# Twelve units: the products of P with the values, and the 64-row products of their items, in quarters of the array

## The chip, the cores and the metric

The kernel runs on one core of a Trainium2 chip. The time is device microseconds (us) of one execution. A profile is one such execution taken by the hardware profiler; it lists every instruction with start and duration, and its span runs from the first to the last of them.

## The reference

An mLSTM cell is followed by a feed-forward layer. The cell has 4 batch rows, 8 heads, 768 tokens and 40 features a head. For each token, with a running maximum m of the gates,

```
m_new  = max(f + m, i);  fs = exp(f + m - m_new);  is = exp(i - m_new)
C      = fs * C + is * v k^T        (40 x 40 a head)
nvec   = fs * nvec + is * k
y      = sigmoid(o) * (C q) / max(|nvec . q|, 1)
```

The outputs of all heads, 320 features a token, make x with 3072 rows. Then h = x @ w_in (320 x 2048), g = h - tanh(h), out = g @ w_out (2048 x 320), all in float32.

## The kernel before, in words

**Units.** The recurrence is cut into chunks of 128 tokens. A unit is one chunk of one batch row; there are 24. Within a unit the cell becomes matmuls: scores `ps` = k q (by head, masked to the causal half and kept as P in SBUF, 128 key tokens by 128 query tokens), P times the scaled values `vs` (whose 41st column is the scaled ones of the normaliser), plus the old state times q. A product of keys and values, `pc`, updates the state for the same batch row's next chunk.

**Items.** The feed-forward runs in items: a group of two units (256 tokens) with one or two pairs p of 128-wide blocks of the 2048 hidden features. `up` (L1015) makes h of an item: w_in's 320 rows are cut in 128, 128 and 64, so each of the two blocks of a pair gets two full products of 128 rows (`full`) and one of 64 rows. The 64-row ones (`rest`) of the two blocks lie in the upper and the lower half of the array's rows and run at the same time. `shrink_steps` (L1036) evaluates g from the PSUM banks ph0 and ph1 by ScalarE (`z`, `q`) and VectorE (`gt`); `sums_of_g` (L888) makes four sums `s1` to `s4` of quarters of g on VectorE, so that `down_seven` (L903) does the second product with seven instead of eight block products, in the banks `pS`. The second product of an item is done while the next item is under way (`LAG` = 1).

**Two schedules.** Units 0 to 11 and the items of the first four groups are ordered by a planner (`Plan`, L157) with a cost for each step. From the item `START` = 17 on, a plain loop (L1497) writes out each item: the full products of `up`, then its 64-row products and, in every other item, the scores of the next unit (L1506), then the second product of the item before. Steps of other engines are put between by a counted clock (`Clock.later`, L141), and each engine runs its instructions in exactly this order.

**Units 12 to 23.** They run in the loop, one in two items. In the item after its scores, a unit gets `block_turned` (L764) between the 64-row products and the second product. It computes the cell's output turned round (features on partitions, tokens along the row) in two banks `turned[0]`, `turned[1]` (`pT` in the profile), one for each half of the heads. Its three parts on TensorE:

- eight products of the old state with q: 40 rows, 64 columns, one in each quarter of the array at a time (L772 to L777);
- eight products of the values with P: 128 rows, 64 columns, so two at a time, in the two column halves (L778 to L784);
- eight products for `pc`, 128 rows and 64 columns too, unless the chunk is the last of its batch row (L785 to L792). Units 20 to 23 have none.

At 1.2 us of the counted clock after that, `turn_back` (L801) transposes both banks in blocks of 32 x 32 on VectorE into `zt`, and SyncE's queue sends them through DRAM (`h_rows`) and reads them back as tokens by features (`z_in`). `gate_turned` (L819) divides and gates in the next unit's slot, and `turn_by_store` (L735) takes the result through DRAM to `xT`. `keep_halves` (L794) updates the state.

**What sets the order on TensorE.** All its instructions are chained in program order (`T.keep`, L120), so a product that waits holds up all that follow. A float32 matmul of the program shows as two MATMUL and two LDWEIGHTS records. The helper lines L106, L129 and L133 record all instructions, so the profile is read by tiles: `ph_up` (item's first product), `pT` (turned output), `pc`, `pS` (second product), `s` and `gt` as above.

Of the kernel before, what the change touches and what calls it, by code (L numbers as in the profile page):

```python
# [49 lines left out]
FP = mybir.dt.float32  # L50
# [5 lines left out]
OP = mybir.AluOpType  # L56
# [4 lines left out]
L = 128  # L61
# [18 lines left out]
def kernel(  # L80
# [33 lines left out]
    V, A, SP, G = Pinned(nc.vector), Pinned(nc.scalar), Pinned(nc.sync), Pinned(nc.gpsimd)  # L114
# [155 lines left out]
    D1 = D + 1  # L270
# [6 lines left out]
    NK = 2  # L277
    HALF = 64
# [6 lines left out]
    HH = H // 2  # L285
# [11 lines left out]
    NX = FIRST + 2  # L297
# [4 lines left out]
    att = ctx.enter_context(tc.tile_pool(name="att", bufs=2))  # L302
# [4 lines left out]
    ps_a = ctx.enter_context(tc.tile_pool(name="ps_a", bufs=1, space=PSUM))  # L307
# [4 lines left out]
    def small(shape, name):  # L312
        banks.append(banks.pop(0))
        return ps_b.tile(shape, FP, name=name, tag=banks[-1])
# [5 lines left out]
    w_in = const.tile([128, NP, WP], FP, name="w_in")  # L320
# [3 lines left out]
    xT = [const.tile([128, NK + 1, TG], FP, name=f"xT{i}") for i in range(NX)]  # L324
# [256 lines left out]
    un = {}  # L581
# [72 lines left out]
    def halves(*parts):  # L654

        for first in (0, 1):
            for steps in parts:
                for step in steps[first]:
                    step()
# [72 lines left out]
    BLOCK = 32  # L732
# [31 lines left out]
    def block_turned(n):  # L764

        t = un[n]
        G.memset(t["wide"][:, H * D1:], 0.0)
        t["turned"] = [ps_a.tile([128, 2, L], FP, name="pT", tag=f"a{i}") for i in range(2)]  # L770
        old = state[t["b"]][(t["c"] + 1) % 2].rearrange("p h d -> p (h d)")
        for g in range(2):  # L772
            for c in range(2):
                for i in range(2):
                    rows, j = slice(i * HALF, i * HALF + D), 2 * g + c
                    T.matmul(t["turned"][i][c * HALF:(c + 1) * HALF, g, :], old[rows, j * D1:j * D1 + HALF], t["qz"][rows, j, :],
                             start=(g == 0), stop=False, skip_group_check=True)  # L777
        for i in range(2):  # L778
            for g in range(2):
                for c in range(2):  # L780
                    j = 2 * g + c
                    at = (i * HH + j) * D1
                    T.matmul(t["turned"][i][c * HALF:(c + 1) * HALF, g, :], t["wide"][:, at:at + HALF], t["P"][:, i, j, :],
                             start=False, stop=True, skip_group_check=True)  # L784
        if n + B < NU:  # L785
            t["pc"] = small([128, HH, D1], "pc")
            k_flat = t["k"].rearrange("p h d -> p (h d)")
            for j in range(HH):
                for i in range(2):
                    h = i * HH + j  # L790
                    T.matmul(t["pc"][i * HALF:(i + 1) * HALF, j, :], k_flat[:, h * D:h * D + HALF], t["vs"][:, h, :],
                             start=True, stop=True, skip_group_check=True)  # L792
# [8 lines left out]
    def turn_back(n):  # L801


        t = un[n]
        zt = att.tile([128, HH * L // BLOCK, BLOCK], FP, name="zt", tag="P", bufs=4)
        flat = zt.rearrange("p b i -> p (b i)")
        for i in range(2):
            V.transpose(flat[:, i * 2 * L:(i + 1) * 2 * L], t["turned"][i].rearrange("p g t -> p (g t)"))
        rows = dram.tile([2, 2, HH, L, BLOCK], FP, name="h_rows", tag=f"h_rows{n % 4}")
        for a in range(128 // BLOCK):  # L810
            half, low = divmod(a, 2)
            SP.dma_start(out=rows[low, half].rearrange("g (b k) i -> k (g b) i", k=BLOCK), in_=zt[a * BLOCK:(a + 1) * BLOCK])
        t["z"] = att.tile([L, 2, H, BLOCK], FP, name="z_in", tag="P", bufs=4)
        for i in range(4):
            part = slice(i * BLOCK, (i + 1) * BLOCK)
            SP.dma_start(out=t["z"][part].rearrange("t a h i -> t (a h) i"),
                         in_=rows.rearrange("a c g t i -> t (a c g) i")[part])
# [55 lines left out]
    def in_seven(g, p):  # L873

        return g >= FIRST or p >= SPLIT
# [136 lines left out]
        r0 = row_of(n)  # L1012
        Clock.later("sent", wait, lambda: A.dma_start(out=out[r0:r0 + L, :], in_=ob))

    def up(some, shrink):  # L1015

        n = len(some)
        ph = [ps_h.tile([128, 2, TG], FP, name="ph_up", tag=f"ph{i}") for i in range(2)]

        def product(i, x, j):  # L1020
            g, p = some[x]
            f = 2 * p + i
            at = ((0, 2, 1), (0, 1, 2))[i][j]
            if j < NK:
                col = (i, 3 - i)[j]
                lhs, rhs = w_in[:, p, col * 128:(col + 1) * 128], xT[g % NX][:, at, :]
            else:
                rows = slice(i * HALF, (i + 1) * HALF)
                lhs, rhs = w_in[rows, p, 2 * NK * 128:], xT[g % NX][rows, at, :]
            T.matmul(ph[i][:, x, :], lhs, rhs, start=(x == 0 and j == 0), stop=(j == NK), skip_group_check=True)  # L1030

        full = [(0.43, lambda i=i, x=x, j=j: product(i, x, j)) for i in range(2) for x in range(n) for j in range(NK)]
        rest = [lambda i=i, x=x: product(i, x, NK) for x in range(n) for i in range(2)]
        return full, (rest, [lambda: shrink(some, ph)])

    def shrink_steps(x, some, ph):  # L1036
# [45 lines left out]
    def shrink(x):  # L1082
        def steps(some, ph):
            n = len(some)
            square, again, cube, product = shrink_steps(x, some, ph)
            for step in (square, again):
                for i in range(2):
                    step(i)
            for i in range(2):
                Clock.later(some, 0.9 + 0.35 * n * i, lambda i=i: cube(i))  # L1090
                Clock.later(some, 1.0 + 0.75 * n + 0.35 * n * i, lambda i=i: product(i))
            if x == len(items) - 1:
                Clock.later("count", 1.0 + 0.36 * n, over_bound)
            if in_seven(*some[0]):
                Clock.later(some, 1.01 + 1.1 * n, lambda: sums_of_g(some))

        return steps
# [56 lines left out]
    while sum(map(len, items)) < len(pairs):  # L1154
        x = sum(map(len, items))
# [64 lines left out]
    of_tokens, of_states, exponentials, rows = {}, {}, [], []  # L1220
# [131 lines left out]
    for p in range(SPLIT, NP):  # L1352
        steps = []
        op = None
        for i in range(2):
            op = plan.add("V", 0.65, lambda p=p, i=i, steps=steps: [steps.extend([] if i else sums_of_weights(p)), *[step() for _, step in steps[2 * i:2 * i + 2]]],
                          [op] if op else [converted[p, 1], *([made[p - 1]] if p % 2 else [converted[n, k] for n in range(1, NP) for k in range(2)])], -7.7512 + -3.8283 * p)
        made[p] = op

    def plan_item(x):  # L1360
# [6 lines left out]
        def begin_item():  # L1367
            busy.append(x)
            got.extend(up(some, lambda some, ph: got.append(shrink_steps(x, some, ph))))
# [109 lines left out]
    def spread_over(steps, x0, x1):  # L1479

        for i, (cost, step) in enumerate(steps):
            at = x0 + i * (x1 - x0) / len(steps)
            work[int(at)].append((at, cost, step))
# [13 lines left out]
    for x in range(START, len(items) + LAG):  # L1497
        dense, new, scored = [], [], news
        for slot, x0, x1 in begins[x]:
            spread_over(cell_slot(*slot), x0, x1)  # L1500
            if slot[0] is not None:
                new.append(slot[0])
        if x < len(items):
            some = tuple(run[:2] for run in items[x])
            dense, rest = up(some, shrink(x))
            dense.append((0.6 + 0.9 * len(new[:1]), lambda: halves(rest, *(scores(n) for n in new[:1]))))  # L1506
            for n in scored:
                dense.append((1.9, lambda n=n: [block_turned(n), Clock.later("turned", 1.2, lambda: [turn_back(n), n + B < NU and keep_halves(n)])]))
        dense += [(0.9, lambda n=n: halves(scores(n))) for n in new[1 if x < len(items) else 0:]]
        some = tuple(run[:2] for run in items[x - LAG])  # L1510
        if in_seven(*some[0]):
            dense += down_seven(some)
        else:
            for i, run in enumerate(items[x - LAG]):
                dense += down(i, some, *run)
        if x == len(items):
            dense.insert(4, (0.0, count))
            dense.insert(13, (0.0, load_count))
        news = new
        merge(dense, [(at - x, cost, step) for at, cost, step in sorted(work[x], key=lambda w: w[0])])  # L1520
# [87 lines left out]
    lead, root, _, rest = POLY  # L1608
# [17 lines left out]
    with tc.If(loaded[0] > 0):  # L1626
# [17 lines left out]
        for g in range(NG):  # L1644
# [19 lines left out]
            for p0 in range(0, NP, 2):  # L1664
# [5 lines left out]
                for p in (p0, p0 + 1):  # L1670
                    for i in range(2):
                        for tt in range(GT):
                            T.matmul(ob[tt], gts[i][:, p - p0, tt * L:(tt + 1) * L], w_out[:, 2 * p + i, :],
                                     start=(p == 0 and i == 0), stop=(p == NP - 1 and i == 1))
# [45 lines left out]
```

## Time and profile before

| what | value |
|---|---|
| median of 3 runs | 521.77 us (521.42 to 532.6) |
| the profiled execution's own time | 523.67 us |
| its span, first to last instruction | 522.0 us |
| TensorE busy (PE) | 512.8 us, 98% |
| VectorE busy (DVE) | 368.4 us, 71% |
| ScalarE busy (ACT) | 200.6 us, 38% |
| granted TensorE clock, mean | 0.995 |

In the profile, PE is TensorE's matmuls and PEld its weight loads. A line of a timeline gives the start, the length, the engine, and how many records of one kind follow each other; "128*64 128x128" is 128 rows and 64 columns of weights and a moving operand of 128 partitions by 128. A busy TensorE is not one at its peak: what counts is the distance between the starts of successive matmuls, since they are pipelined.

### The profile page before, as it was taken

Reading aid. Unit: us, or ns where it says so; the run is one execution under the profiler, and the core shown is the slowest. Engines: PE = TensorE matmul, PEld = TensorE weight load, DVE = VectorE, ACT = ScalarE, POOL = GpSimd, SP = SyncE. Lnnn points to the kernel's source line nnn. Section 1 sums busy time; section 2 is a strip of 40 time slices with the busy share of each in tenths; the row PEclk is TensorE's granted clock in tenths of the full one; section 3 lists DMA queues with packets and bytes.
Section 4 is the critical chain, followed back from the end, with each engine's and each line's share of the span. In section 5 each row is a group of like instructions: output and inputs, shape, how many; then the busy total and the mean of one; then the engine's idle time right before and its main releaser. Section 6 shows DMA issues by size and latency. Waiting matters only on the chain.

```text
span 522.0 us, 9917 instructions
## 1 busy us (share of the span) xinstructions
PE 512.8 (98%) x3705; PEld 442.4 (85%) x3705; DVE 368.4 (71%) x828; ACT 200.6 (38%) x511; POOL 38.3 (7%) x75
## 2 busy tenths in 40 slices
PE   9999999999999999999999999999999999999995
PEld 5778888887898888898898898898888888898984
DVE  5899979998855657786767667668658658663734
ACT  4465697676434242231321331232232232232321
POOL 5423224120000000000000000000000000000000
PEclk9899999999999999999999999999999999999999
DMA  7987646431003000042533533534433432310001
GB/s 228 285 245 227 180 141 193 131 111 33 3 3 91 6 27 26 4 108 50 133 64 89 147 67 85 129 69 87 107 77 85 107 79 36 80 31 1 26 1 31
DMA packets 100383, 47.29 MB, mean 91 GB/s; under 512 B 75048, under 2 KB 94056, under 8 KB 100328
## 3 DMA queue, kind: packets, MB, share of 16 engines
q1 hardware_dynamic: 94096, 31.84, 25.3%
q0 software_dynamic: 3040, 10.82, 6.6%
q10 hardware_dynamic: 3192, 3.93, 2.2%
q8 instruction: 31, 0.51, 0.4%
q14 instruction: 24, 0.20, 0.1%
HBM read 36.91 MB, written 9.44 MB: 89 GB/s over the span
## 4 chain that ended last, share of the span: by engine, by line
PE 94%; DMA 3%; ACT 1%; POOL 1%; DVE 0%; issue 0%; SPq 0%; DVEq 0%
PE ph_up L129 42%; PE pS L129 31%; PE po L129 7%; PE ph L129 4%; PE pT L129 4%; PE ps L129 4%; PE pc L129 2%; DMA w<-in_moe_w_in 2%; PE px L133 1%; DMA w_out<-in_i_gate 0%; POOL w L106 0%; ACT vs L106 0%; PE awake L129 0%; ACT L106 0%; DVE w_in L106 0%
## 5 line engine op out<-in xcount | busy, mean ns | idle before, releaser
L129 PE MATMUL ph_up<-xT,w_in 128*128 128x256 f32 (+1 forms) x1152 | 228.9, 388 | 0.0
L129 PEld LDWEIGHTS ph_up<-xT,w_in 128*128 128x128 f32 (+1 forms) x1152 | 176.2, 189 | 35.5 <-issue 15.3
L106 ACT ACTIVATE z<-ph_up 128x512 f32<-128x512 f32 (+1 forms) x98 | 56.8, 583 | 254.2 <-issue 123.7
L106 DVE SCALAR_TENSOR_TENSOR gt<-ph_up,z 128x512 f32<-128x512 f32 (+1 forms) x98 | 63.5, 675 | 68.0 <-ACT z L106 67.6
L129 PE MATMUL pS<-wT,s 128*128 128x160 f32 x480 | 72.0, 299 | 0.0
L129 PEld LDWEIGHTS pS<-wT,s 128*128 128x128 f32 x480 | 67.4, 190 | 0.0
L106 ACT ACTIVATE q<-z,tiny 128x512 f32<-128x512 f32 (+1 forms) x98 | 66.3, 711 | 1.0
L106 DVE SCALAR_TENSOR_TENSOR gt<-q,gt 128x512 f32<-128x512 f32 (+1 forms) x98 | 63.2, 676 | 0.0
L106 DVE TENSOR_TENSOR P<-ps,upto 128x512 f32<-128x512 f32 x36 | 23.3, 686 | 52.9 <-PE ps L129 52.8
L129 PE MATMUL pS<-w_out,gt 128*128 128x160 f32 x320 | 54.3, 312 | 0.0
L129 PEld LDWEIGHTS pS<-w_out,gt 128*128 128x128 f32 x320 | 44.6, 189 | 7.5 <-issue 3.6
L129 PE MATMUL po<-w_out,gt 128*128 128x320 f32 x128 | 38.2, 441 | 0.0
L129 PEld LDWEIGHTS po<-w_out,gt 128*128 128x128 f32 x128 | 23.1, 190 | 8.5 <-issue 0.3
L106 DVE TENSOR_TENSOR s<-gt 128x256 f32<-128x256 f32 x80 | 30.2, 418 | 0.0
L129 PE MATMUL pS<-w_out,s 128*128 128x160 f32 x160 | 28.3, 299 | 0.0
L129 PE MATMUL pS<-wT,gt 128*128 128x160 f32 x160 | 28.3, 299 | 0.0
L129 PEld LDWEIGHTS ps<-qz,kz 40*128 40x128 f32 x384 | 25.7, 190 | 2.1 <-issue 0.7
L129 PE MATMUL ps<-qz,kz 40*128 40x128 f32 x384 | 26.5, 276 | 0.0
L129 PEld LDWEIGHTS ph<-vs,P 128*128 128x128 f32 x192 | 23.9, 192 | 1.6 <-POOL P L106 1.2
L129 PE MATMUL ph<-vs,P 128*128 128x41 f32 x192 | 24.4, 273 | 0.7 <-POOL P L106 0.7
L129 PEld LDWEIGHTS pS<-w_out,s 128*128 128x128 f32 x160 | 23.9, 190 | 0.0
L129 PEld LDWEIGHTS pS<-wT,gt 128*128 128x128 f32 x160 | 23.9, 190 | 0.0
(105 smaller groups left out, 475.6 us busy)
## 6 DMA issues: line engine op xcount, KB each, us to landing
w<-in_moe_w_out POOLq DMA_DIRECT2D x8, 640.0 KB, 6.2
w<-in_moe_w_in POOLq DMA_DIRECT2D x16, 256.0 KB, 4.7
kz<-in_kT SPq DMA_DIRECT2D x48, 80.0 KB
o<-in_o_gate SPq DMA_DIRECT2D x24, 160.0 KB
k<-in_k SPq DMA_DIRECT2D x20, 180.0 KB
qz<-in_qT SPq DMA_DIRECT2D x44, 80.0 KB
v<-in_v SPq DMA_DIRECT2D x22, 160.0 KB
out<-ob ACTq DMA_DIRECT2D x11, 320.0 KB
```

The source lines that it names most:

```text
L106: i = method(*args, **kwargs)
L129: return cls.keep(nc.tensor.matmul(*args, **kwargs))
L133: return cls.keep(nc.tensor.transpose(*args, **kwargs))
```

## The change

It touches four places, for units 12 to 23 and their items alone.

- `block_turned`: the products of the values with P are cut along the key tokens in two halves of 64 rows, sixteen instead of eight, each in a quarter of the array. The bank now goes by the token half r, so each of the two banks has four blocks (head half i and g) instead of two, and the state's products go where they were by partition, at block `i * 2 + g`. The sum over the token halves is no longer made in PSUM.
- `update_halves`: the part of `block_turned` that makes `pc`, as a function of its own; nothing else changes in it.
- `turn_back`: ScalarE copies bank 1 (128x512) to SBUF, VectorE adds bank 0 to it, and one transpose of 128x512 takes the place of two of 128x256. The new buffer `both` holds `zt` and the sum; it is as large as the other tiles of its tag `P`.
- `up`: a new argument `quarters`. In the items where a unit has its `block_turned` (`scored` not empty), each 64-row product of 64x128 is made as two of 64x64, one for each column half.

```diff
+        t["turned"] = [ps_a.tile([128, 2 * 2, L], FP, name="pT", tag=f"a{i}") for i in range(2)]
         for g in range(2):
             for c in range(2):
                 for i in range(2):
                     rows, j = slice(i * HALF, i * HALF + D), 2 * g + c
-                    T.matmul(t["turned"][i][c * HALF:(c + 1) * HALF, g, :], old[rows, j * D1:j * D1 + HALF], t["qz"][rows, j, :],
+                    T.matmul(t["turned"][i][c * HALF:(c + 1) * HALF, i * 2 + g, :], old[rows, j * D1:j * D1 + HALF], t["qz"][rows, j, :],
                              start=(g == 0), stop=False, skip_group_check=True)
         for i in range(2):
             for g in range(2):
                 for c in range(2):
-                    j = 2 * g + c
-                    at = (i * HH + j) * D1
-                    T.matmul(t["turned"][i][c * HALF:(c + 1) * HALF, g, :], t["wide"][:, at:at + HALF], t["P"][:, i, j, :],
-                             start=False, stop=True, skip_group_check=True)
+                    for r in range(2):
+                        rows, j = slice(r * HALF, (r + 1) * HALF), 2 * g + c
+                        at = (i * HH + j) * D1
+                        T.matmul(t["turned"][r][c * HALF:(c + 1) * HALF, i * 2 + g, :], t["wide"][rows, at:at + HALF], t["P"][rows, i, j, :],
+                                 start=False, stop=True, skip_group_check=True)
+        update_halves(n)
+
+    def update_halves(n):
+        t = un[n]
         if n + B < NU:
             t["pc"] = small([128, HH, D1], "pc")
...
-        zt = att.tile([128, HH * L // BLOCK, BLOCK], FP, name="zt", tag="P", bufs=4)
+        both = att.tile([128, 2, HH * L // BLOCK, BLOCK], FP, name="zt", tag="P", bufs=4)
+        zt, added = both[:, 0], both[:, 1].rearrange("p b i -> p (b i)")
         flat = zt.rearrange("p b i -> p (b i)")
-        for i in range(2):
-            V.transpose(flat[:, i * 2 * L:(i + 1) * 2 * L], t["turned"][i].rearrange("p g t -> p (g t)"))
+        A.copy(out=added, in_=t["turned"][1].rearrange("p g t -> p (g t)"))
+        V.tensor_tensor(out=added, in0=t["turned"][0].rearrange("p g t -> p (g t)"), in1=added, op=OP.add)
+        V.transpose(flat, added)
...
-    def up(some, shrink):
+    def up(some, shrink, quarters=False):
...
+        def quarter(i, x, c):
+            g, p = some[x]
+            rows, cols, first = slice(i * HALF, (i + 1) * HALF), slice(c * HALF, (c + 1) * HALF), 2 * NK * 128 + c * HALF
+            T.matmul(ph[i][cols, x, :], w_in[rows, p, first:first + HALF], xT[g % NX][rows, ((0, 2, 1), (0, 1, 2))[i][NK], :],
+                     start=False, stop=True, skip_group_check=True)
+
         full = [(0.43, lambda i=i, x=x, j=j: product(i, x, j)) for i in range(2) for x in range(n) for j in range(NK)]
-        rest = [lambda i=i, x=x: product(i, x, NK) for x in range(n) for i in range(2)]
+        if quarters:
+            rest = [lambda i=i, x=x, c=c: quarter(i, x, c) for x in range(n) for c in range(2) for i in range(2)]
+        else:
+            rest = [lambda i=i, x=x: product(i, x, NK) for x in range(n) for i in range(2)]
...
-            dense, rest = up(some, shrink(x))
+            dense, rest = up(some, shrink(x), bool(scored))
```

More of the change, by code (lines that the diff above doesn't have):

```diff
@@ L769, in block_turned @@
         G.memset(t["wide"][:, H * D1:], 0.0)
-        t["turned"] = [ps_a.tile([128, 2, L], FP, name="pT", tag=f"a{i}") for i in range(2)]
         old = state[t["b"]][(t["c"] + 1) % 2].rearrange("p h d -> p (h d)")
+        t["turned"] = [ps_a.tile([128, 2 * 2, L], FP, name="pT", tag=f"a{i}") for i in range(2)]
         for g in range(2):
```

## The prediction

> **What bounds the kernel now.** I read the page's busy shares first, then the waits of 217 to 522 us, then the timeline of single items. The page:
>
> ```profile
> span 522.0 us, 9917 instructions
> PE 512.8 (98%) x3705; PEld 442.4 (85%) x3705; DVE 368.4 (71%) x828; ACT 200.6 (38%) x511; POOL 38.3 (7%) x75
> PE 94%; DMA 3%; ACT 1%; POOL 1%; DVE 0%; issue 0%; SPq 0%; DVEq 0%
> ```
>
> TensorE is the chain that ends last. Who waits, in the stretch of units 12 to 23 and after:
>
> ```profile
> DVE P L106 <- PE ps L129: 47.7, 11, 4.7
> DVE gt L106 <- ACT z L106: 44.6, 20, 4.6
> PEld ph_up L129 <- issue: 10.3, 31, 0.3
> PEld pT L129 <- issue: 6.0, 24, 0.3
> PEld pS L129 <- DVE gt L106: 0.7, 4, 0.2
> ```
>
> VectorE and ScalarE wait for TensorE; TensorE's matmuls wait for nobody. What is left on the weight loads is "issue", at most some 0.33 us at a time, 24 times at `pT`. So the change is worth what it does to TensorE's own sequence. Its weight loads in the item of unit 12 (the last row is cut by the window):
>
> ```profile
> 217.98 0.73 PEld L129 LDWEIGHTS ph_up<-xT,w_in 64*128 64x128 f32 x8 [0.33 <-issue]
> 219.05 0.42 PEld L129 LDWEIGHTS pT<-qz,state 40*64 40x64 f32 x16 [0.33 <-issue]
> 219.65 0.85 PEld L129 LDWEIGHTS pT<-P,vs 128*64 128x64 f32 x16 [0.17 <-issue]
> 220.46 0.60 PEld L129 LDWEIGHTS pc<-vs,k 128*64 128x64 f32 x16
> 221.12 0.30 PEld L129 LDWEIGHTS pS<-w_out,gt 128*128 128x128 f32 x2
> ```
>
> The idle notes stand exactly where the shape of the array changes (64x128, quarters, 128x64); from P to `pc`, both 128x64, there is none, and `pc`'s loads even start ahead of its first matmul at 220.57. From start to start the stages take 1.065 us (64-row products), 0.597 (state), 0.924 (P), 0.545 (`pc`).
>
> **Splitting each stage.** The starts of single records give the steps. In steady flow a 256-column matmul follows after 0.216 us, a 160-column one after 0.136, a 128-column one after 0.109, whether one runs or two or four in parts of the array (the state's quarters come four together every 0.109). `pc`, with 41 columns, comes two every 0.058. Above that:
> - leaving a shape: 217.676 + 0.216 = 217.892, but the 64-row products start at 217.985: 0.093. Likewise 0.097 before the state, 0.110 before P, 0.115 between `pc` and `pS`; about 0.10 between P and `pS` in units 20 to 23, which have no `pc`.
> - the first step in a new shape is longer: 0.320 instead of 0.216 with weights of 128 columns (+0.104), 0.160 instead of 0.109 with 64 columns (+0.051).
>
> All twelve units show these to 0.002 us.
>
> **What the Trainium skill says.** "TensorEngine Tiling (Array Packing)", Key Properties: changing the tiling mode, not just the tile, drains TensorE. The trace agrees, 0.09 to 0.12 us a change. "TensorE: Matmul & The Clock Gate", section LDWEIGHTS: a load takes its columns over 1.2 GHz, so 0.107 us for 128 and 0.053 for 64. That is the longer first step (0.104, 0.051): after a drain the first load is exposed. It is also `pc`'s 0.058. The first page's Restrictions and Gotchas say that different row tiles must not use one PSUM bank at the same time, which is why a token half needs its own bank; no run here shows it, and the state's row halves write to two banks already.
>
> **The change part by part.**
> 1. *64-row products in quarters.* 8 records in 4 pairs of 0.216 become 16 in 4 rounds of four: the streaming, 0.863, stays. The drain before it stays. The first step has 64-column weights: +0.051 instead of +0.104. Behind it the state is in the same shape, so 0.097 goes. 1.065 becomes 0.863 + 0.051 = 0.914: −0.151. Four quarters with 256 columns are not in the trace; bounds for the first step are 0.051 and 0.104 (the old one), no gain beyond, since a load can't be shorter than 64 columns take.
> 2. *State.* Both its first step (+0.051) and the drain behind it (0.110) go: 0.597 becomes 4 x 0.109 = 0.437: −0.160.
> 3. *P.* 16 records in 8 pairs become 32 in 8 rounds of four: the same 0.873. The first step (0.051) goes. With `pc` behind it, a change from quarters to 128x64 comes in, 0.110 as between state and P now: 0.924 becomes 0.983, +0.059. Without `pc` the drain to `pS` was there already: −0.051.
> 4. *`pc`* now stands behind a drain. Its first load is exposed (0.053) and its short first steps (0.036, 0.051) become 0.058: last start after 0.053 + 7 x 0.058 = 0.459 instead of 0.379, so +0.080. The trace has no such entry with 41 columns; bounds 0.03 (only part of the load exposed) and 0.13 (first step as long as P's 0.160 instead of 0.036).
> 5. *Copy and sum.* ScalarE gets a 128x512 copy from PSUM (0.579 by `P<-ps`) a unit; it is issued after both `q`, which end at 241.7 in unit 13, when P's products are long done. VectorE gets an addition of 128x512 (0.686 by its row of `P<-ps,upto`) and one transpose of 512 columns for two of 256. From SBUF, `yt<-ys` took 0.446 for 256 columns and 0.267 for 128, so about 0.80 for 512, against 0.77 for the pair now. Together +0.7 us of VectorE. Queued behind it there: the state update, the second `gt`, the four `s`. In unit 13 that `gt` ends at 244.45 and its matmul starts at 250.52; the last `s` ends at 246.11, used at 252.26. The tightest unit (12) has 3.7 us. The banks of `ph` are read by the cubes ahead of it. `zt` would be ready at about 244.0, SyncE issues its stores at 246.86, being held by `xT<-y_rows`; only unit 12 stores at once, and its `z_in` ends at 229.4, read at 236.3. So it costs nothing; without cover it would be 0.7 x 12 = 8.4 us.
> 6. *The rest.* `update_halves`, the larger buffer and the indices issue nothing new. No DMA is added or moved. Units 0 to 11 and the tail keep their code.
>
> Sum: with `pc` −0.151 − 0.160 + 0.059 + 0.080 = −0.172, eight times −1.38; without, −0.151 − 0.160 − 0.051 = −0.362, four times −1.45. Together **−2.8 us**. With the bounds: item 1 up to +0.053 x 12 = +0.6, item 4 ±0.05 x 8 = ±0.4, so −1.8 to −3.2. Against the profiled execution's own 523.67 this gives 520.9; that one lies 1.9 above the median, so against the median, 521.77, I forecast **519.0 us** for the timed runs.
>
> **Rivals.**
> - *Slower: the supply of instructions.* From the 64-row products to the end of `pc` there are now 16 + 16 + 32 + 16 = 80 pairs of load and matmul in 2.96 us, against 56 in 3.13. If dispatch takes d a pair and a full queue of 64 instructions ("TensorE: Matmul & The Clock Gate", the table of specs at its head) holds 32 pairs at the start, d decides from 2.96/48 = 0.062 us on. The same page, section "Wait — 56ns, not 53.3ns?", has 0.062 us per matmul where the sequencer's program decodes; which decoding runs here no view shows. The trace only caps d: no 1230 consecutive pairs came faster than 0.119 us each after taking off 32. At d = 0.10 a unit with `pc` takes 4.8 instead of 2.96, so +1.84 − 0.17 = +1.67, eight times 13.4; the others 32 x 0.10 − 2.31 − 0.36 = +0.53, four times 2.1: **537 us**. Against it: the state's four pairs a step of 0.109, and `pc`'s 0.029 a pair at the end of 48 pairs, with no sign of slowing beyond the load's own 0.053.
> - *VectorE's extra reaches TensorE.* 521.77 − 2.8 + 8.4 = **527 us**, against slack of at least 3.7 us in every unit.
> - *The shape change isn't what is saved.* If the waits (on banks, q, state) at the state's first loads caused that drain, only steps 2's exit and the entries would go and `pc` would lose: −0.097 x 12 = 1.2 less gain, **520.2 us**. Against: the same 0.093 stands before the 64-row products, whose loads await no semaphore.
>
> **Chances.** Forecast 0.82; change of shape not saved in full 0.08; VectorE 0.04; supply 0.06. One measurement can tell about 2% (10.4 us) from no change. Only the supply case passes that, and only for d well over 0.062: slower 0.04; faster 0.01; same 0.95. Range: the forecast's −1.8 to −3.2 gives 518.6 to 520.0, the timed runs scatter by some 0.3 to 0.5 about it, and the reach toward the smaller gain sets the upper end: 517.7 to 521.2.
>
> **What would show it.** `pT<-qz,state` right behind the 64-row products, 0.437 from start to start of P, and no idle note at either; a new one of some 0.17 at `pc`; 32 records of `pT<-P,vs` in about 0.87 to their drain; items with a unit shorter by 0.17 or 0.36, all others unchanged. Wrong: rounds of quarters over 0.109 (0.216 for 256 columns), or a matmul of `pS` waiting for `gt` or `s`.

## The result

The changed kernel takes 518.3 us (median of six, 517.73 to 518.37) where the kernel before, with its runs on the same chip, takes 521.69: a ratio of 0.9935, with a 95% interval of 0.9922 to 0.9949. That is 3.4 us less, 2.7 to 4.1 by the interval. 519.0 had been forecast, with a range of 517.7 to 521.2. Some executions take about 10 us longer than the others, whatever the kernel, and the ratios leave them out.

The page of the profile after (its own time 518.27 us) has the same lines as the one before:

```profile
span 516.6 us, 10519 instructions
PE 507.4 (98%) x3993; PEld 440.1 (85%) x3993; DVE 375.5 (73%) x828; ACT 206.1 (40%) x523; POOL 37.8 (7%) x75
PE 94%; DMA 2%; ACT 1%; POOL 1%; DVE 0%; issue 0%; SPq 0%; DVEq 0%
```

TensorE has 288 more matmul records and is still busy for 5.4 us less (not all of that is the change's, see below); VectorE and ScalarE have 7.1 and 5.5 us more. The chain is TensorE as before. The waits of 211 to 516 us:

```profile
DVE P L106 <- PE ps L129: 37.8, 11, 3.7
DVE gt L106 <- ACT z L106: 43.9, 20, 4.6
PEld ph_up L129 <- issue: 10.3, 31, 0.3
PEld pS L129 <- issue: 3.0, 11, 0.3
PEld pc L129 <- issue: 1.4, 8, 0.2
```

The 24 waits at `pT` are gone, and eight short ones at `pc` have come, one for each unit that has a `pc`. The weight loads of unit 12's item show it in place:

```profile
216.14 0.64 PEld L129 LDWEIGHTS ph_up<-xT,w_in 64*64 64x64 f32 x16 [0.33 <-issue]
216.84 0.59 PEld L129 LDWEIGHTS pT<-qz,state 40*64 40x64 f32 x16
217.39 0.92 PEld L129 LDWEIGHTS pT<-P,vs 64*64 64x64 f32 x32
218.48 0.55 PEld L129 LDWEIGHTS pc<-vs,k 128*64 128x64 f32 x16 [0.17 <-issue]
219.08 0.43 PEld L129 LDWEIGHTS pS<-w_out,gt 128*128 128x128 f32 x3
```

One idle note is left on the way in and one at `pc`; the state's and P's loads start ahead of their matmuls, as `pc`'s alone did before. In units 20 to 23, where `pS` follows P, the lines before (first two) and after are:

```profile
379.62 0.85 PEld L129 LDWEIGHTS pT<-P,vs 128*64 128x64 f32 x16 [0.17 <-issue]
380.64 0.43 PEld L129 LDWEIGHTS pS<-w_out,gt 128*128 128x128 f32 x3 [0.17 <-DVE gt L106]
375.79 0.92 PEld L129 LDWEIGHTS pT<-P,vs 64*64 64x64 f32 x32
376.88 0.57 PEld L129 LDWEIGHTS pS<-w_out,gt 128*128 128x128 f32 x4 [0.17 <-issue]
```

P begins without an idle note after the change, and the note at `pS` stays.

**A stretch that can be compared.** The two spans differ by 5.4 us, more than the change did. The difference up to the eleventh group of full products, where the code is the same, is not the change's: the kernel before reaches that group at 79.72 us, the changed kernel at 77.88 in this profile and at 79.72 in a later one (`after_again`). In the profile before, a load of w_in landed 0.7 us later and the clock was 0.91 from 20 to 40 us. From that group to the first unit's item both kernels take 134.72. So all kernels below are compared by the stretch from the start of the first unit's item to the start of the last item, in which each stage of a unit repeats from unit to unit to 0.003 us. Views of that stretch before and after (length and busy time by engine, with the records in brackets, clock, share and rate of transfers):

```profile
214.44:502.83 288.39, 288.39 (x2250) 255.00 (x2249) 193.25 (x454) 81.66 (x209) 0.95 (x8) 1.00 0.33 75
```

```profile
212.60:498.03 285.43, 285.43 (x2539) 254.23 (x2537) 200.51 (x454) 87.32 (x221) 0.94 (x8) 1.00 0.34 76
```

288.39 − 285.43 = **2.96 us**, with full clock in both and TensorE busy throughout. By stages, each taken between starts, in all twelve units alike:

| stage | before | forecast | after |
|---|---|---|---|
| 64-row products | 1.064 | 0.914 | 0.914 |
| state | 0.598 | 0.437 | 0.439 |
| P, with `pc` behind it | 0.924 | 0.983 | 0.986 |
| `pc` | 0.545 | 0.625 | 0.596 |
| P, with `pS` behind it | 1.025 | 0.974 | 0.986 |

"`pc` behind it" holds for units 12 to 19, "`pS` behind it" for 20 to 23. With `pc` that is 3.131 − 2.935 = 0.196 a unit, without 2.687 − 2.339 = 0.348; 8 x 0.196 + 4 x 0.348 = 2.96. The rest of the 3.4 in the timed runs lies within their interval.

### The profile page after: what moved, and what is told of

Its sections match the earlier page's. It is cut to its first block, busy times and chain, and to the rows that moved or that the text cites. A ratio compares the mean times of both kernels' runs of the same rounds, so it can differ in the third digit from the quotient of the medians.

```text
span 516.6 us, 10519 instructions
## 1 busy us (share of the span) xinstructions
PE 507.4 (98%) x3993; PEld 440.1 (85%) x3993; DVE 375.5 (73%) x828; ACT 206.1 (40%) x523; POOL 37.8 (7%) x75
## 4 chain that ended last, share of the span: by engine, by line
PE 94%; DMA 2%; ACT 1%; POOL 1%; DVE 0%; issue 0%; SPq 0%; DVEq 0%
PE ph_up L129 42%; PE pS L129 31%; PE po L129 7%; PE ph L129 4%; PE ps L129 4%; PE pT L129 3%; PE pc L129 2%; DMA w<-in_moe_w_in 2%; PE px L133 1%; DMA w_out<-in_i_gate 0%; POOL w L106 0%; ACT vs L106 0%; PE awake L129 0%; ACT L106 0%; DVE w_in L106 0%
## 5 line engine op out<-in xcount | busy, mean ns | idle before, releaser
L129 PE MATMUL ph_up<-xT,w_in 128*128 128x256 f32 (+2 forms) x1248 | 227.5, 387 | 0.0
L129 PEld LDWEIGHTS ph_up<-xT,w_in 128*128 128x128 f32 (+2 forms) x1248 | 173.6, 180 | 36.3 <-issue 15.3
```

Of the source, the lines that this page charges most:

```text
L129: return cls.keep(nc.tensor.matmul(*args, **kwargs))
```

## The experiments

Theory: each change of the array's shape costs TensorE a drain (the gap, beyond the usual step, between the last matmul in the old shape and the first in the new one) and the time of the first weight load after it; the change saves some of these, and nothing else of it reaches the end. Rivals: P's quarters themselves gain; the semaphores of the first loads were what stood there; VectorE's extra work costs; the supply of instructions does. Where the timed runs are too scattered for a narrow interval, the stretch decides.

**Only the 64-row products in quarters** (e1), on the kernel before, with `up` as in the change. The blocks for the state, P and the transposes are those of before.

```diff
-            dense, rest = up(some, shrink(x))
+            dense, rest = up(some, shrink(x), bool(scored))
```

> Only the 64-row products of the twelve items in quarters; P with values, banks and transposes as before. Theory (changes of the array's shape): the 64-row products go from 1.065 to 0.914 us, the state from 0.597 to 0.547 (its first step no longer pays a weight load, its drain to 128x64 stays), P and pc unchanged: -0.201 x 12 = -2.4 us, about 519.3 us. That is over 80% of the whole gain, without a copy or a sum. Rival (the gain sits in P's quarters and the second bank): no gain, about 521.7.

Two of its four timed runs took 520.1 and 520.7 us, the other two 530.4 and 531.1; that gives no interval. The stretch took 286.00, 2.39 less than before: 64-row products 0.914, state 0.548, P and `pc` unchanged.

```profile
216.67 0.64 PEld L129 LDWEIGHTS ph_up<-xT,w_in 64*64 64x64 f32 x16 [0.33 <-issue]
217.37 0.59 PEld L129 LDWEIGHTS pT<-qz,state 40*64 40x64 f32 x16
218.13 0.85 PEld L129 LDWEIGHTS pT<-P,vs 128*64 128x64 f32 x16 [0.17 <-issue]
218.95 0.60 PEld L129 LDWEIGHTS pc<-vs,k 128*64 128x64 f32 x16
```

The note is at P now, not at `pc`. Four fifths of the gain need no second bank, copy or sum.

**Only the cell's part** (e2), on the changed kernel: P in quarters, banks by token half, copy and sum.

```diff
-            dense, rest = up(some, shrink(x), bool(scored))
+            dense, rest = up(some, shrink(x))
```

> Only P with the values in quarters, a bank for each token half, copy and sum; the 64-row products stay 64x128. Theory: the drain between state and P goes (state 0.597 to 0.488), but the same drain appears between P and pc (P 0.924 to 0.985, pc 0.545 to 0.596): +0.003 in the eight units with pc, -0.15 in the four without: -0.6 us, about 521.1, hardly to be told from before. Rival (gain in P's quarters): about 519.

Ratio to before 0.9978 (0.9956 to 1.0). Stretch 287.81, 0.58 less: state 0.488, P 0.986, `pc` 0.596, so nothing in the eight units with `pc` and 0.149 in the four others.

```profile
215.59 0.73 PEld L129 LDWEIGHTS ph_up<-xT,w_in 64*128 64x128 f32 x8 [0.33 <-issue]
216.66 0.43 PEld L129 LDWEIGHTS pT<-qz,state 40*64 40x64 f32 x16 [0.33 <-issue]
217.04 0.92 PEld L129 LDWEIGHTS pT<-P,vs 64*64 64x64 f32 x32
218.13 0.55 PEld L129 LDWEIGHTS pc<-vs,k 128*64 128x64 f32 x16 [0.17 <-issue]
```

The two parts sum to 2.39 + 0.58 = 2.97: they act apart from each other.

**P in quarters in the last four units alone** (e3), the 64-row products in all twelve, on the changed kernel. The condition stands in `block_turned` and `turn_back`; its first branch is the code before the change, the other that after it.

```diff
+        if n + B < NU:
...
+        else:
...
```

> The 64-row products in quarters in all twelve items, but P in quarters with copy and sum only in the four units without pc. Theory: -0.201 x 8 - 0.348 x 4 = -3.0 us, 518.7: the same as the whole change (-3.0 by its trace), since with pc behind it a quartered P only moves the drain. Rival (each quartered P gains): 0.5 to 1 us slower than the whole change.

Ratio to before 0.9962 (0.9941 to 0.9984); stretch 285.41 against 285.43 of the whole change. Where `pc` follows, quartering P moves the drain behind P and brings nothing; the copy, the sum and the second bank are work for nothing there.

**Two changes of shape more, and nothing else** (e4), on the kernel before:

```diff
             dense, rest = up(some, shrink(x))
+            ahead = rest[0][:2]
+            del rest[0][:2]
+            dense.insert(6, (0.0, lambda ahead=ahead: [step() for step in ahead]))
```

> The kernel before, but in the loop's 32 items the 64-row products of the item's first pair stand ahead of the last two full products: no product, wait or buffer is added, only two more changes of shape in each item. Theory: 0.093 + 0.104 on the way in and 0.097 + 0.104 on the way out = 0.40 us an item, 32 times: +12.7 us, about 534.5. Rival (what stood at these places were the semaphores of the first loads): no change, 521.7.

Ratio 1.0245 (1.0194 to 1.0297), that is 10.1 to 15.5 us slower. The profiled execution is one of the long ones (span 543.4), but its stretch has the full clock: 30 of the 32 items take 300.35 against 288.40, so 11.95 more, or 0.398 an item; 0.40 was expected.

```profile
226.87 0.73 PEld L129 LDWEIGHTS ph_up<-xT,w_in 128*128 128x128 f32 x4 [0.33 <-issue]
227.93 0.30 PEld L129 LDWEIGHTS ph_up<-xT,w_in 64*128 64x128 f32 x4 [0.33 <-issue]
228.56 0.42 PEld L129 LDWEIGHTS pT<-qz,state 40*64 40x64 f32 x16 [0.33 <-issue]
```

At 226.87 the same full products of the same item come back, on data that were there before, and still pay. The records of these products await no semaphore (nor do those at 227.93). The semaphore rival is out: the price goes with the shape.

**Three and ten sums more** (e5, e6), on the changed kernel. They add load on VectorE alone; `flat` is overwritten by the transpose. The diff is that of e5; e6 has 10 for 3.

```diff
         A.copy(out=added, in_=t["turned"][1].rearrange("p g t -> p (g t)"))
+        for _ in range(3):
+            V.tensor_tensor(out=flat, in0=t["turned"][0].rearrange("p g t -> p (g t)"), in1=added, op=OP.add)
         V.tensor_tensor(out=added, in0=t["turned"][0].rearrange("p g t -> p (g t)"), in1=added, op=OP.add)
```

> The changed kernel with three more additions of 128x512 in each of the twelve units, ahead of the one that counts (they write to where the transpose writes later). Theory: 3 x 0.69 = 2.1 us more on VectorE a unit, against slack of 2.6 us in unit 12 and over 5 us in the others: no change, 518.3. Rival (VectorE's extra reaches TensorE): 2.1 x 12 = +25 us.

> Ten more additions a unit, 6.9 us of VectorE, more than the 5.2 us from the end of the second gt to its matmul. Theory: TensorE now waits about 6.9 - 5.2 = 1.7 us a unit and 4 us in unit 12, some 20 us in all, about 538; the waits show as pS waiting for gt. Rival (cover is much larger than read): no change.

With three, the stretch is 285.43, to 0.01 us that of the changed kernel (ratio to before 0.9908, 0.9871 to 0.9945). 2.1 us a unit more is hidden, and so 0.6 is. With ten the ratio is 1.069 (1.0636 to 1.0744), the stretch 324.93: +39.5, double what I had expected, and the first thing late was not the one that I had named. In unit 13's next item:

```profile
249.00 5.77 DVE L106 TENSOR_TENSOR zt<-pT,zt 128x512 f32<-128x512 f32 x8
252.72 0.73 PEld L129 LDWEIGHTS ph_up<-xT,w_in 64*128 64x128 f32 x8 [0.33 <-issue]
254.84 1.09 PEld L129 LDWEIGHTS ps<-qz,kz 40*128 40x128 f32 x16 [1.38 <-PE ph_up L129]
```

The sums (eight of eleven in the window) hold the `pT` banks until 254.77, and the next unit's scores, which go into the same banks, start at 254.84 instead of about 253.7. Only after that do `gt` and `s` come late. I had read the cover off the uses of `gt` and `s`. Compared stage by stage with the changed kernel, 20.9 of the 39.5 us are the eleven late starts of scores, each 1.2 to 3.5 us late. The clock has a part too, as the page shows (40 slices of the span):

```profile
PEclk9999999999999999799979989999999899999999
```

It is granted at half rate in four stretches, two of 6.8 us (from 230.0 and 277.8) and two of 3.4 (from 325.6 and 438.2): 20.5 us, in which some 10 are lost by estimate. The remaining 8 to 9 lie in later stages, where among others `pS` once waits 2.4 us for `gt`. So the bank's wait is the first and the largest term, but half of the 39.5 comes behind it.

**`pc` for two units at once** (e7), on the changed kernel: units 12 and 13, 14 and 15, and so on, after the second of them.

```diff
     def update_halves(n):
-        t = un[n]
-        if n + B < NU:
-            t["pc"] = small([128, HH, D1], "pc")
+        if n + B >= NU or n % 2 == 0:
+            return
+        both = small([128, 2, HH, D1], "pc")
+        for m in (n - 1, n):
+            t = un[m]
+            t["pc"] = both[:, m % 2]
...
-... n + B < NU and keep_halves(n) ...
+... n + B < NU and n % 2 and [keep_halves(n - 1), keep_halves(n)] ...
```

> The changed kernel with the pc products of units 12 to 19 made for two units at once, after the second. Theory: in every other unit P is followed by pS at once, so pc's visit to 128x64 with its exposed load and drain (0.596 - 8 x 0.058 = 0.13 us) goes four times: -0.5 us against the changed kernel, 517.8. Rival: the longer life of k and vs, or the later state, holds something up: slower by a few us.

Ratio to before 0.9922 (0.99 to 0.9944). Stretch 284.91, 0.52 less than the changed kernel: two `pc` take 1.063 together, P with `pS` behind it 0.986.

```profile
237.87 1.01 PEld L129 LDWEIGHTS pc<-vs,k 128*64 128x64 f32 x32 [0.17 <-issue]
238.93 1.11 PEld L129 LDWEIGHTS pS<-w_out,gt 128*128 128x128 f32 x8
```

Nothing is held up by the longer life of k and vs.

**Quarters in all items of the loop, scores too** (e8), on the changed kernel.

```diff
-            T.matmul(ps[i][:, j, :], t["kz"][rows, j, :], t["qz"][rows, j, :], start=True, stop=True)
+            if PLANNED <= n and not t.get("decays"):
+                for c in range(2):
+                    cols = slice(c * HALF, (c + 1) * HALF)
+                    T.matmul(ps[i][cols, j, :], t["kz"][rows, j, cols], t["qz"][rows, j, :], start=True, stop=True, skip_group_check=True)
+                return
+            T.matmul(ps[i][:, j, :], t["kz"][rows, j, :], t["qz"][rows, j, :], start=True, stop=True)
...
-            dense, rest = up(some, shrink(x), bool(scored))
+            dense, rest = up(some, shrink(x), True)
```

> The changed kernel with quarters in all 32 items of the loop, the scores of units 12 to 23 too (sixteen 64x64 products for eight of 64x128). Theory: streaming stays, the first step after the full products pays a weight load of 64 columns instead of 128 in the 20 other items: -0.053 x 20 = -1.1 us against the changed kernel, 517.2. Rival (supply of instructions: 48 more pairs in each item with scores... 24 more loads and 24 more matmuls): rounds of quarters longer than 0.109, slower by some us.

Ratio 0.9889 (0.9842 to 0.9937). Stretch 284.52, 0.91 less than the changed kernel. The 64-row products take 0.914 ahead of scores (0.968 before); without scores 1.024 ahead of `pS` (1.064), since leaving quarters drains for 0.110, not 0.097. The scores, 32 records for 16, go on at the old pace (0.985 for 0.989). Eleven items of the stretch have scores and seven have neither scores nor a unit: 11 x (0.054 + 0.004) + 7 x 0.040 = 0.92, which is the 0.91 measured within rounding.

```profile
230.00 0.64 PEld L129 LDWEIGHTS ph_up<-xT,w_in 64*64 64x64 f32 x16 [0.33 <-issue]
230.70 1.03 PEld L129 LDWEIGHTS ps<-qz,kz 40*64 40x64 f32 x32
231.90 1.11 PEld L129 LDWEIGHTS pS<-w_out,gt 128*128 128x128 f32 x8 [0.17 <-issue]
```

**Both, and both with the planned part in quarters too** (e9, e10), beside the changed kernel once more. e10 passes `True` in the planner's call of `up` as well and quarters the scores of units 0 to 11.

> Both earlier edits together: pc for two units at once, and quarters in all 32 items of the loop with the scores of units 12 to 23. Theory (each is a change of shape less or a cheaper one, so they add): -0.5 - 0.9 = -1.4 us against the changed kernel between the first unit's item and the last item, 284.0 where that had 285.4. Rival (they share what they save): no more than -0.9.

> As the kernel with both edits, and the planned part too makes its 64-row products and the scores of units 0 to 11 in quarters. Theory: 0.053 us less at each entry into the 64-row shape, some 25 to 30 of them before 212 us, less 0.013 for a longer drain: -1.0 to -1.5 us before the first unit's item; less if that part waits for weights and transfers rather than for TensorE. Rival (supply of instructions): the planned part gets slower by several us.

> The changed kernel unaltered, beside the two others on one chip. Theory: 0.6% under the kernel before, 285.4 us between the first unit's item and the last item, as in its first profile.

| kernel | ratio to before, 95% | stretch, us |
|---|---|---|
| changed | 0.9929 (0.9908 to 0.9949) | 285.43 |
| pairs and quarters | 0.9885 (0.9848 to 0.9923) | 283.99 |
| and in the planned part | 0.9889 (0.985 to 0.9929) | 284.00 |

285.43 − 283.99 = 1.44: the two edits add (0.52 + 0.91). Between the eleventh group of full products and the first unit's item e10 takes 134.12, e9 134.66 and the changed kernel 134.72. So the planned part in quarters brings 0.54 more there, short of the 1.0 to 1.5 expected for the whole planned part. What it brings in the first 80 us is open: the other profiled executions reach the eleventh group between 77.3 and 81.4 us with the same code (88.4 in e4's), more than the edit could bring. The best of e10's six timed runs was 515.4 us, e9's 516.1, the changed kernel's on that chip 517.4. Both versions beat the kernel before by their intervals and, by the stretch, the changed one; the intervals of the timed runs overlap.

## Why the prediction was right

- **Bound.** TensorE without a wait in the whole stretch, before and after: so a difference in its sequence is a difference in time. Right.
- **Items 1 and 2** (64-row products, state) came out to 0.002 us: −0.150 and −0.159 against −0.151 and −0.160. e1 and e2 show each entry and exit alone.
- **Item 3** (P): +0.062 with `pc` against +0.059; without, −0.039 against −0.051, as the drain out of quarters into full rows is 0.11, not the 0.10 seen out of 128x64.
- **Item 4** (`pc`) is the mis-sized term: +0.051, not +0.080, inside the bounds given. I had added a whole exposed load of 0.053 and lost both short first steps. The starts after the first one came after 0.080 and then every 0.058 (last 0.430, forecast 0.459): only 0.022 of the load shows in front of 41 columns. Eight times 0.029 is 0.23 us more gain than in the sum (−2.82); items 1 to 3 together gave 0.10 less, and what is left is the 0.14 by which −2.96 exceeds it. The drain behind `pc` is also misread: with the step of 0.058 it is 0.108, not 0.115, in both kernels, and drops out of the difference.
- **Item 5** (copy and sum) is hidden, shown by e5. The copy took 0.577, the sum 0.679 and the transpose 0.711 (0.80 expected); VectorE's busy time in the stretch rose by 7.26 us, 0.6 a unit. The cover I named was the wrong one: e6 shows that the banks are wanted first. So this item's result was right with a reason that would have failed under more load.
- **The timed runs.** 518.3 lies 0.65 under the forecast: 0.14 of it is the sum's and 0.08 the baseline's (521.69 for 521.77); the rest is below what these runs resolve. That the errors of item 4 and of items 1 to 3 have opposite signs and partly cancel is luck.
- **Rivals.** Supply of instructions: with `pc` in pairs 96 pairs of load and matmul come at 0.035 us each, and the quarters of P keep 0.109 for four through all eight rounds. Even with 32 of them queued beforehand, as the prediction allowed, 64 pairs in 3.4 us cap the dispatch at 0.053 a pair, under the 0.062 from which it would decide. "TensorE: Matmul & The Clock Gate" (section "Wait — 56ns, not 53.3ns?") in the Trainium skill states about 0.062 us per matmul only for the case that the sequencer's program decodes; these runs stay under that figure, so it does not bind them. VectorE's extra: out by e5. The semaphores: out by e4.
- **Tiling page.** "TensorEngine Tiling (Array Packing)" in the Trainium skill, Key Properties, says that a change of mode drains TensorE; e4 puts 0.398 us on a pair of changes with 128-column weights, drains and first loads together.

## What to carry to other kernels

Where TensorE never waits, count its changes of array shape: in this float32 kernel each cost a drain of 0.09 to 0.11 us plus the first weight load (0.10 us with 128 columns, 0.05 with 64). Where a finer cut streams as fast, cut products so that neighbours have one shape. But follow the shape to the end of the row: a product that is recut only to be followed by one of the old shape only moves the drain (e3), and its extra copies and sums buy nothing. Read the cover of added work off the first use of every buffer it holds, the PSUM banks too, not off its results alone.

## What the runs showed of the hardware that I had not expected

- Four quarters of the array, each with its own load and matmul, keep 0.109 us a round of 128 columns for twelve rounds on end (state and P of the changed kernel): 0.027 us a pair of load and matmul.
- The first load after a drain costs its full length ahead of a long matmul (0.051 for 64 columns) but 0.022 ahead of one with 41 columns, whose steps are as long as a load (0.058) anyway.
- With ten sums more, which make TensorE pause, the granted clock was 0.90 between 212 and 245 us and 0.97 after 275, where the stretch of the kernels without pauses had 1.00. Within that it was 0.50 from 231.0 to 236.6 us, behind the first pause of 3.5 us. Each of the four stretches at half rate begins in a pause of 2 us or more or within about 1 us after it, but others of that length (near 369 and 413 us) passed without one. That the pauses caused it was not tried by itself.
